# Start of a fused attention and feed-forward kernel: warm-up matmuls, halved first loads, and another order of the weight loads

## The chip, the core and the metric

The kernel runs on one core of a Trainium2 chip. The metric is the device time of one execution in microseconds (us). The core has five engines with their own instruction streams: TensorE (PE; its weight loads are listed as PEld), VectorE (DVE), ScalarE (ACT), GpSimd (POOL) and SyncE (SP). DMAs are issued by POOL or SP and are carried by the core's 16 DMA engines.

## The reference

```python
def _attn_ref(q, k, v):                       # q, k, v: (8, 8, 576, 64)
    scores = np.matmul(q, k.transpose(0, 1, 3, 2)) / np.sqrt(64)
    rel = pos[:, None] - pos[None, :]
    mask_plain = (rel >= 0) & (rel < 32)                          # heads 0 to 3
    mask_dil = (rel >= 0) & (rel < 128) & (rel % 4 == 0)          # heads 4 to 7
    scores = np.where(mask, scores, -1e9)
    attn = softmax(scores)
    return np.matmul(attn, v)

x = attn_out.transpose(0, 2, 1, 3).reshape(4608, 512)
h = x @ w_in                                  # 512 x 2048
g = h * sigmoid(beta * h)
out = g @ w_out                               # 2048 x 512
```

All inputs and the output are float32; the kernel computes its products in bfloat16.

## The kernel before

The work has two halves. Attention is done for one batch of 576 tokens at a time and leaves its result, transposed, in `xT`. The feed-forward part runs over nine tiles of 512 tokens (`NTT`). Its weights stay in SBUF: `w_in_bf` is loaded in four DMAs of 512 columns, `w_out_bf` in four quarters of 512 rows. Every load that casts from float32 to bfloat16 is issued by POOL.

Attention is cut into small steps whose order is written out by hand as lists of names: `FIRST` for batch 0, `SECOND` for batch 1, `THIRD` for batch 2 and `STEPS` for the others. In a name the letter is the kind and the digits are the head pair and the part. Head pairs 0 and 1 are the plain ones, 2 and 3 the dilated ones.

- `K` and `Q` (batches 0 and 1 only) transpose rows of k and q, which lie with tokens on partitions in `tok`, by TensorE into PSUM, and copy them out (`transposes_d`, `transposes_p`, `step_k`, `step_q`).
- `S` computes a block of scores and its exponential on ScalarE. For batches 0 and 1 the mask is added by a matmul with `neg_d` or `neg_p`; later batches multiply by a mask on POOL.
- `V` multiplies with the values and divides by the sums on VectorE. `X` transposes the result and ScalarE copies it into `xT`.
- `v0` and `v1` cast the two parts of the dilated values from `vd_st` into `vd`, `v2` casts the plain values from `vp_st` into `vp` (`cast_v`). `H0` and `H1` start the first two feature blocks of tile 0 from the half of `xT` that is there.

For batches 2 to 7, q and k take another way: POOL issues a DMA that casts them into a scratch tensor in DRAM (`cast_qk`, the tensor `qk`), and SP then issues DMA transposes of it (`load_dil`, `load_plain`), which are spread into place by copies (`d`, `k`, `q` in the lists).

The main loop goes over the nine tiles. A tile has 16 slots `slot_h` (four matmuls on `w_in_bf`, a tanh on ScalarE, then `g` on VectorE) and 16 slots `slot_o` (token block `tb`, part 0 to 3; a part is four matmuls on one quarter of `w_out_bf`). Between the slots of tile t stand the attention steps of batch t + 1. In tile 0 the steps of batch 1 begin after the tenth slot, and the order of the `slot_o` is part by part, so that each quarter of `w_out_bf` is used by three token blocks before the next one is needed:

```python
left = [(slot_o, 0, tb, part) for part in range(4) for tb in range(3)] + left[12:]
```

Every engine works through its instructions in the order in which they are written. POOL's order before the main loop is: the loads of batch 0 (dilated k and q, dilated v, plain k and q, plain v) with the identity and the `neg` masks in between, `w_in_bf`, the cast `v2`, the first two quarters of `w_out_bf`, the loads of batch 1, the two `cast_qk` of batch 2, the last two quarters of `w_out_bf`, then memsets and masks.

Of the kernel before, what the change touches and what calls it, by code (L numbers as in the profile page):

```python
# [20 lines left out]
).split()  # L21

FIRST = (
    "K2 K3 Q2 S20 S21 v0 S22 S23 v1 S30 S31 K0 K1 S32 V20 S33 V21 Q0 V22 V23 S00 V30 "
    "S01 V31 X20 S02 v2 V32 S10 V33 X21 S11 V00 X30 S12 V01 X31 V10 H0 X00 V11 H1 X01 X10 X11"
).split()
SECOND = (
    "K2 K3 Q2 v0 S20 v1 S21 S22 S23 K0 K1 S30 V20 S31 Q0 V21 S32 V22 S33 V23 V30 S00 "
    "V31 X20 v2 S01 V32 S02 V33 S10 X21 S11 V00 X30 S12 V01 X31 V10 X00 V11 X01 X10 X11"
).split()  # L30
THIRD = (
# [6 lines left out]
def kernel(  # L38
# [10 lines left out]
    nc = tc.nc  # L49
# [15 lines left out]
    NFB = DFF // P  # L65
    NTOK = 512
    NTT = B * S // NTOK
    WG = 512
    FROM = {1: 2}
    DV = D + 2  # L70
    NEG = 1e9
# [19 lines left out]
    def bank(dt=FP32):  # L91
        b = psum_at.tile([P, 512], FP32, name="at")
        return b[:] if dt == FP32 else b[:].bitcast(BF16)
# [35 lines left out]
    for n, x in ((n, x) for x in (1, 0) for n in "kq"):  # L129
        R, T = (48, 12) if x else (64, 9)  # L130
        tok[n, x] = xT[0:R, :, c:c + T * D]
        c += T * D
    warm = const([P, 1], FP32, "warm")
    gate_t = const([1, 16], BF16, "gate_t")


# [2 lines left out]
            nc.gpsimd.memset(kz[i][64:128, :, :, 0], 0.0)  # L139
            nc.gpsimd.memset(kz[i][0:64, :, :, 1], 0.0)  # L140

    def zeros(i):
        if i == 0:
            for x in range(4):
                nc.vector.memset(pt[x][:, pt_w[x]:], 0.0)
            for x in range(2, 4):
                nc.vector.memset(pt[x][64:96, 8 * DQ[0]:8 * DQ[0] + 32], 0.0)
        nc.vector.memset(qzd[i][64:128, 0], 0.0)
        nc.vector.memset(qzd[i][0:64, 1], 0.0)
        nc.vector.memset(vd[i][:, :, :, :, D:D + 1], 1.0)  # L150
        nc.vector.memset(k1[i][:, :, 0:WIN], 0.0)
        nc.vector.memset(q1[i][64:128, :, 0], 0.0)
        nc.vector.memset(q1[i][0:64, :, 1], 0.0)
        nc.vector.memset(vp[i][:, :, :, D:D + 1], 1.0)


    def band(flat, w, lo, hi, yes, no):
        nc.gpsimd.memset(flat, yes)
        if len(flat.shape) == 2:
            flat = flat.unsqueeze(1)  # L160
        r = flat.shape[1]
        nc.gpsimd.affine_select(
            out=flat, in_=flat, pattern=[[0, r], [1, w]], base=-lo,
            channel_multiplier=-1, compare_op=ALU.is_ge, fill=no)
        nc.gpsimd.affine_select(
            out=flat, in_=flat, pattern=[[0, r], [-1, w]], base=hi,
            channel_multiplier=1, compare_op=ALU.is_ge, fill=no)
# [4 lines left out]
    def build_neg_d():  # L172
        for hf, lo in enumerate(LO):
            band(neg_d[hf][:], DQ[hf], -lo, WIN - 1 - lo, 0.0, -NEG)


    def build_neg_p():
        band(neg_p[:], QT, -WIN, -1, 0.0, -NEG)
        nc.gpsimd.memset(neg_p[0:WIN, 0], -NEG)
# [28 lines left out]
        nc.vector.tensor_single_scalar(  # L208
            out=beta_half[:], in_=tpb[:, 0:NFB], scalar=0.5, op=ALU.mult)

    def load_w_in(g):
        nc.gpsimd.dma_start(
            out=w_in_bf[:, :, g * WG:(g + 1) * WG],
            in_=moe_w_in[:, g * WG:(g + 1) * WG].rearrange("(c p) d -> p c d", p=P))

    def load_w_out(g):
        nc.gpsimd.dma_start(
            out=w_out_bf[:, g * 4:(g + 1) * 4, :],
            in_=moe_w_out[g * 4 * P:(g + 1) * 4 * P, :].rearrange("(c p) d -> p c d", p=P))
# [12 lines left out]

    def load_tok(b, n, x):
        dst = tok[n, x]
        R, T = (48, 12) if x else (64, 9)
        src = {"q": q, "k": k}[n][b, 4 * x:4 * x + 4].rearrange("h (a T) d -> a h (T d)", T=T)
        nc.gpsimd.dma_start(out=dst, in_=src)


    def load_dil(b, kind):
# [18 lines left out]
    def copy_on(eng):  # L261
        return eng.copy if eng is nc.scalar else eng.tensor_copy
# [21 lines left out]
    def load_vp_1(b, eng, n=0, m=4 * NI, p=0):  # L284
        eng.dma_start(
            out=vp_st[b % 2][:].rearrange("p h i d -> p (h i) d")[p:P, n:n + m],
            in_=bass.AP(tensor=v.tensor, offset=v[b, 0].offset + (QT * n - WIN + p) * D,
                        ap=[[D, P - p], [QT * D, m], [1, D]]))
# [11 lines left out]
    def load_vd(b, eng):  # L300
        rows = v[b, 4:8].rearrange("h (t T) d -> t h (T d)", T=C)
        st = vd_st[:].rearrange("p f h T d -> p f h (T d)")
        for hf in range(2):
            eng.dma_start(out=st[0:DK[hf], hf], in_=rows[DO[hf]:DO[hf] + DK[hf]])


    def cast_v(b, n, eng):
        if n == 2:
            copy_on(eng)(out=vp[b % 2][:, :, :, 0:D], in_=vp_st[b % 2][:])
        else:  # L310
            f, K = (slice(n, n + 1), DK[n]) if n < 2 else (slice(0, 2), 96)
            copy_on(eng)(
                out=vd[b % 2][0:K, f].rearrange("p f h T e -> p (f h T) e")[:, :, 0:D],
                in_=vd_st[0:K, f].rearrange("p f h T d -> p (f h T) d"))
# [3 lines left out]
        kd[b] = kd_pool.tile([P, 2, 4, CT], BF16, name="kdT")  # L318


    def transposes_d(n, rp):
        src = tok[n, 1]
        tv = bank(BF16)[:, 0:4 * CT].rearrange("p (h w a) -> p h w a", h=4, w=3)
        for h4 in range(4):
            for w in range(3):
                c = (4 * w + 2 * rp) * D
                nc.tensor.transpose(tv[:, h4, w], src[:, h4, c:c + 2 * D], ident_b[0:48, 0:48])
        return tv.rearrange("p h w a -> p h a w")


    def transposes_p(n, x):
        src = tok[n, 0]
        tv = bank(BF16)[:, 0:S].rearrange("p (e a) -> p e a", e=9)
        for h2 in range(2):
            for e in range(9):
                nc.tensor.transpose(
                    tv[64 * h2:64 * h2 + 64, e], src[:, 2 * x + h2, e * D:(e + 1) * D],
                    ident_b[0:64, 0:64])
        return tv.rearrange("p e a -> p a e")

    def step_k(b, x):
        eng = nc.scalar if x % 2 else nc.vector
        if x < 2:
            copy_on(eng)(out=k1[b][:, x, WIN:].rearrange("p (a e) -> p a e", e=9),
                         in_=transposes_p("k", x))
        else:
            copy_on(eng)(out=kd[b][:, x - 2].rearrange("p h (a w) -> p h a w", w=3),
                         in_=transposes_d("k", x - 2))


    def step_q(b, x):
        tv = [transposes_p("q", y) if y < 2 else transposes_d("q", y - 2) for y in (x, x + 1)]
        for n, hf in ((0, 0), (1, 1), (0, 1), (1, 0)):
            y, rows = x + n, slice(64 * hf, 64 * hf + 64)
            out = (q1[b][rows, y, hf].rearrange("p (a e) -> p a e", e=9) if x < 2 else
                   qzd[b][rows, hf, y - 2].rearrange("p h (a w) -> p h a w", w=3))
            copy_on(nc.scalar if hf else nc.vector)(out=out, in_=tv[n][rows])  # L357

    def step_s(b, x, j):
# [88 lines left out]
            nc.scalar.copy(out=o, in_=xp[:, 0:m * n].rearrange("p (T t) -> p T t", T=C))  # L448

    STEP = {"K": step_k, "Q": step_q, "S": step_s, "V": step_v, "X": step_x}  # L450
    BRING = {"d": spread_dil, "k": spread_k, "q": spread_q, "v": cast_v}

    def attention_step(b, name):
        if name[0] == "H":
            slot_h(0, int(name[1:]), (2, 3))
        elif name[0] in STEP:
            STEP[name[0]](b, *[int(c) for c in name[1:]])
        else:
            eng = (nc.scalar if name[0] == "v" and (b, name) in ((1, "v2"), (2, "v0"), (2, "v1"), (2, "v2")) else
                   nc.gpsimd if b == 0 and name == "v2" else nc.vector)  # L460
            BRING[name[0]](b, int(name[1:]), eng)


# [97 lines left out]
    def gate(element):  # L561
        G.tensor_copy(out=gate_t[0:1, 0:1], in_=element)

    V.memset(warm[:], 0.0)
    A.activation(out=warm[:], in_=warm[:], func=ACT.Exp)
    V.memset(vp_st[0][0:WIN, 0, 0], 0.0)
    SQ.dma_start(out=beta_row[:], in_=moe_beta.rearrange("(f p) -> f p", p=P))
    for n in "kq":
        load_tok(0, n, 1)
    make_identity(nc, ident_b[:])  # L570
    load_vd(0, G)
    load_tok(0, "k", 0)
    build_neg_d()
    load_tok(0, "q", 0)
    load_vp_1(0, G, 0, 1, WIN)
    load_vp_1(0, G, 1, 4 * NI - 1)
    build_neg_p()
    for g in range(4):
        load_w_in(g)
    make_identity(nc, ident_f[:])  # L580
    zeros(0)
    for name in FIRST:
        if name == "S11":
            build_beta()
        attention_step(0, name)
    for g in range(2):
        load_w_out(g)
    for x in (1, 0):
        for n in "kq":
            load_tok(1, n, x)  # L590
    G.memset(vd_st[64:96, 1], 0.0)
    load_vd(1, G)
    load_vp_1(1, G)
    for kind in "kq":
        cast_qk(2, kind)
    zeros(1)
    V.memset(plain_T["k"][:, 0:WIN // 2], 0.0)
    for kind in "kq":
        load_dil(2, kind)
    for kind in "kq":  # L600
        load_plain(2, kind)
    for g in range(2, 4):
        load_w_out(g)
    zeros_kz()
    build_masks_d()
    build_masks_p()
# [68 lines left out]
```

## Time and profile before

| | |
|---|---|
| median of 11 runs | 341.63 us (340.9 to 344.13) |
| the profiled execution | 341.39 us |
| its span, first to last instruction | 339.7 us |
| PE busy | 311.1 us (92%) |
| DVE, ACT, POOL busy | 193.3, 197.6, 130.4 us |
| moved by DMA | 42.61 MB, mean 125 GB/s |
| matmul of 128x512 on `w_in_bf` (line 475) | 380 ns, 520 of them |
| matmul of 128x512 on `w_out_bf` (line 508) | 379 ns, 512 on `o_ps` |
| first instruction of PE | 6.72 us |
| PE idle for a DMA, total | 8.3 us for k, 0.9 us for q, 3.1 us for `w_out_bf` |

A duration is that of one instruction. Matmuls overlap in the array: four on `w_out_bf` in a row end 1.02 us after the first starts, and 0.86 us lie between the starts of two such groups. Times in the text are counted from the first instruction of the span; the device time is 1.7 us longer than the span.

### The profile page before, as it was taken

How to read it: one execution, taken by the hardware profiler on the slowest of the kernel's cores; microseconds unless marked ns; L12 is line 12 of the kernel's file. 1: busy time of each engine (PE TensorE's matmuls, PEld its weight loads, DVE VectorE, ACT ScalarE, POOL GpSimd, SP SyncE). 2: the span in 40 equal slices, each digit the busy share in tenths (PEclk: the TensorE clock that was granted, in tenths of full speed). 3: DMA queues.
4: the chain of work that ended last, by engine and by line, in shares of the span. 5: the costliest groups of instructions: out<-in, count | busy, mean ns of one | idle time of the engine just before them, and what ended most of it. 6: DMA issues, size and time to landing. Idle time of an engine off the chain costs nothing.

```text
span 339.7 us, 6278 instructions
## 1 busy us (share of the span) xinstructions
PE 311.1 (92%) x2389; PEld 165.7 (49%) x2389; DVE 193.3 (57%) x424; ACT 197.6 (58%) x374; POOL 130.4 (38%) x170
## 2 busy tenths in 40 slices
PE   1889796997899899999999999999999999999994
PEld 1754463544455455555555555555555444444441
DVE  4588663479657774767386637763865344244400
ACT  2577564686747675666666656665666555355411
POOL 8773594133385346534653465354434000000000
PEclk9999999999999999999999999999999999999999
DMA  7999999999899695979688968892001210011121
GB/s 107 209 206 207 181 229 169 211 209 201 147 162 166 125 188 112 172 181 131 133 140 185 125 134 153 172 126 63 20 13 33 62 33 32 32 31 34 41 82 62
DMA packets 64734, 42.61 MB, mean 125 GB/s; under 512 B 48832, under 2 KB 58976, under 8 KB 64320
## 3 DMA queue, kind: packets, MB, share of 16 engines
q1 hardware_dynamic: 57120, 25.58, 40.0%
q0 software_dynamic: 7584, 16.64, 27.9%
q8 instruction: 18, 0.29, 0.4%
q14 instruction: 12, 0.10, 0.1%
HBM read 39.32 MB, written 16.52 MB: 164 GB/s over the span
## 4 chain that ended last, share of the span: by engine, by line
PE 75%; DMA 12%; DVE 5%; ACT 4%; issue 1%; POOL 1%; ACTq 0%; POOLq 0%
PE o_ps L508 31%; PE h_ps L475 29%; DMA xT<-in_q_dram 7%; DMA w_out_bf<-in_moe_w_out_dram 5%; PE h_ps L508 3%; PE at L417 3%; PE at L434 2%; PE at L391 2%; PE at L384 2%; ACT osb L513 2%; DVE g L485 2%; DVE qq L278 1%; ACT tnh L482 1%; DVE xs L424 1%; POOL pt L399 1%
## 5 line engine op out<-in xcount | busy, mean ns | idle before, releaser
L485 DVE SCALAR_TENSOR_TENSOR g<-tnh,h_ps 128x512 bf16<-128x512 bf16 x130 | 88.8, 685 | 90.4 <-ACT tnh L482 89.6
L475 PE MATMUL h_ps<-xT,w_in_bf 128*128 128x512 bf16 x520 | 131.2, 380 | 2.5 <-DVE g L485 2.1
L508 PE MATMUL o_ps<-w_out_bf,g 128*128 128x512 bf16 x512 | 128.9, 379 | 3.8 <-ACT osb L513 3.8
L482 ACT ACTIVATE tnh<-h_ps,beta_half 128x512 bf16<-128x512 f32 x130 | 89.3, 687 | 56.3 <-PE h_ps L475 51.8
L508 PEld LDWEIGHTS <-g 128*128 128x128 bf16 x576 | 52.3, 97 | 57.4 <-issue 8.3
L475 PEld LDWEIGHTS <-w_in_bf 128*128 128x128 bf16 x576 | 51.8, 98 | 51.5 <-issue 3.5
L397 ACT ACTIVATE pt<-at 128x384 bf16<-128x384 f32 (+2 forms) x112 | 48.4, 439 | 20.8 <-PE at L384 8.5
L399 POOL TENSOR_TENSOR pt<-pt,mask_d 96x384 bf16<-96x384 bf16 (+1 forms) x48 | 36.9, 778 | 52.3 <-ACT pt L397 51.7
L424 DVE TENSOR_TENSOR xs<-at,rcp 96x256 bf16<-96x256 f32 (+2 forms) x96 | 44.5, 463 | 12.3 <-PE at L434 8.4
L399 POOL TENSOR_TENSOR pt<-pt,mask_PP 128x384 bf16<-128x384 bf16 x24 | 22.8, 948 | 37.8 <-ACT pt L397 37.7
L513 ACT ACTIVATE osb<-o_ps 128x512 f32<-128x512 f32 x32 | 19.1, 597 | 23.7 <-PE o_ps L508 23.6
L417 PEld LDWEIGHTS <-pt 128*128 128x128 bf16 (+2 forms) x448 | 24.5, 97 | 13.5 <-DVE xs L424 0.2
L420 DVE RECIPROCAL rcp<-at 96x4 f32<-96x4 f32 (+2 forms) x96 | 16.8, 175 | 8.4 <-PE at L417 7.7
L391 PEld LDWEIGHTS <-kdT 128*96 128x96 bf16 (+1 forms) x128 | 15.3, 127 | 11.9 <-issue 2.3
L391 PE MATMUL at<-qzd,kdT 128*96 128x192 bf16 (+1 forms) x128 | 19.0, 236 | 1.6 <-ACT qzd L357 0.8
L434 PE MATMUL at<-ident_b,xs 96*128 96x96 bf16 (+1 forms) x224 | 18.0, 200 | 1.3 <-DVE xs L424 1.2
L434 PEld LDWEIGHTS <-xs 96*128 96x128 bf16 (+1 forms) x224 | 13.2, 96 | 11.4 <-DVE xs L424 1.9
L417 PE MATMUL at<-vd,pt 96*128 96x65 bf16 (+1 forms) x256 | 18.3, 193 | 0.0
L508 PE MATMUL h_ps<-w_out_bf,g 128*128 128x512 bf16 x64 | 15.5, 379 | 3.1 <-DMA w_out_bf<-in_moe_w_out_dram 3.1
L399 POOL TENSOR_TENSOR pt<-pt,mask_FP 128x384 bf16<-128x384 bf16 x12 | 10.9, 910 | 16.0 <-ACT pt L397 16.0
L448 ACT COPY xT<-at 128x384 bf16<-128x384 bf16 (+1 forms) x32 | 12.6, 394 | 3.9 <-PE at L434 3.9
L444 ACT COPY xT<-at 128x288 bf16<-128x288 bf16 x24 | 9.0, 399 | 10.0 <-PE at L434 10.0
(89 smaller groups left out, 225.3 us busy)
## 6 DMA issues: line engine op xcount, KB each, us to landing
vp_st<-in_v_dram SPq DMA_DIRECT2D x12, 384.0 KB, 8.8
qk<-in_k_dram POOLq DMA_DIRECT2D x6, 576.0 KB, 5.7
qk<-in_q_dram POOLq DMA_DIRECT2D x6, 576.0 KB, 8.7
vd_st<-in_v_dram SPq DMA_DIRECT2D x6, 384.0 KB, 5.2
w_in_bf<-in_moe_w_in_dram POOLq DMA_DIRECT2D x4, 512.0 KB, 11.5
w_out_bf<-in_moe_w_out_dram POOLq DMA_DIRECT2D x4, 512.0 KB, 16.3
out_dram<-osb SPq DMA_DIRECT2D x8, 256.0 KB, 2.6
vd_st<-in_v_dram SPq DMA_DIRECT2D x6, 320.0 KB, 6.4
```

Of the source, the lines that this page charges most:

```text
L391: nc.tensor.matmul(sc[0:K, a, 0:2 * n], lhsT=kd[b][:, rp, h4, DO[hf]:DO[hf] + K], rhs=qzd[b % 2][:, :, rp, h4, hf * DQ[0]:hf * DQ[0] + n], ...
L397: nc.scalar.activation(out=w, in_=sc[0:K, :, 0:2 * n], func=ACT.Exp, scale=SCALE)
L399: nc.gpsimd.tensor_tensor(out=w, in0=w, in1=mask[0:K], op=ALU.mult)
L417: nc.tensor.matmul(pv[:, a, h2, :], lhsT=pt[x][0:K, c:c + P], rhs=rhs, start=True, stop=True)
L420: nc.vector.reciprocal(out=rcp[0:n, 0:m], in_=pv[0:n, :, :, D])
L424: nc.vector.tensor_tensor(out=xs_t[b, x, jx][:, a0:a0 + m], in0=pv[0:n, :, :, 0:D], in1=rcp[0:n, 0:m].unsqueeze(3).to_broadcast([n, m, 2, ...
L434: nc.tensor.transpose(xp[:, a * n:(a + 1) * n], xs[:, a].rearrange("p h d -> p (h d)"), ident_b[0:n, 0:n])
L475: nc.tensor.matmul(hps, lhsT=w_in_bf[:, kt, fb * P:(fb + 1) * P], rhs=xT[:, kt, t * NTOK:(t + 1) * NTOK], start=(kt == 2), stop=(kt == 1))
L482: nc.scalar.activation(out=tnh[:], in_=hps, func=ACT.Tanh, scale=beta_half[:, fb:fb + 1])
L485: nc.vector.scalar_tensor_tensor(out=g[:], in0=tnh[:], scalar=1.0, in1=hps, op0=ALU.add, op1=ALU.mult)
L508: nc.tensor.matmul(ops[:], lhsT=g_t[t, fb][:, tb * P:(tb + 1) * P], rhs=w_out_bf[:, fb, :], start=(fb == 0), stop=(fb == NFB - 1))
L513: nc.scalar.mul(out=osb[:], in_=ops[:], mul=0.5)
```

## The change

1. Matmuls on a tile of zeros (`W10`, `W2`, `W3` and `W2` in `FIRST`, 17 in all) are issued on TensorE before and between the first transposes.
2. The dilated k and q of batch 0 are loaded in two DMAs each, by head pair. `K2`, `Q2`, `K3` and `Q3` become steps of one head pair each, for batch 0 and batch 1, and their copies are half as large.
3. All memsets of VectorE that were spread over two places come first, apart from `z0`, `z1` and `z2`. The memsets of the `neg` masks go from POOL to VectorE.
4. `w_in_bf` is loaded in pieces of 256, 256, 512 and 1024 columns, issued after the cast `v1`, which moves from VectorE to POOL for batch 0. The last piece is issued after the first half of the plain values is cast.
5. The plain values of batch 0 are loaded and cast in two parts (`v4`, `v5`) in place of `v2`, both on POOL.
6. The quarters of `w_out_bf` are issued between the loads of batch 1: the first after its dilated q and k, the second after its plain q and k, the third after its dilated values, and the last after the casts and transposes of batch 2.
7. The lists `FIRST` and `SECOND` are in a new order.

The core of the diff:

```diff
 FIRST = (
-    "K2 K3 Q2 S20 S21 v0 S22 S23 v1 S30 S31 K0 K1 S32 V20 S33 V21 Q0 V22 V23 S00 V30 "
-    "S01 V31 X20 S02 v2 V32 S10 V33 X21 S11 V00 X30 S12 V01 X31 V10 H0 X00 V11 H1 X01 X10 X11"
+    "W10 K2 W2 Q2 W3 K3 S20 S21 Q3 W2 S22 S23 z0 v0 S30 S31 S32 S33 V20 V21 K0 v1 V22 V23 V30 K1 X20 "
+    "V31 Q0 V32 V33 X21 S00 X30 S01 X31 S02 v4 S10 V00 S11 V01 S12 H0 v5 X00 V10 H1 X01 V11 X10 X11 z1 z2"
 ).split()
 SECOND = (
-    "K2 K3 Q2 v0 S20 v1 S21 S22 S23 K0 K1 S30 V20 S31 Q0 V21 S32 V22 S33 V23 V30 S00 "
+    "K2 Q2 K3 Q3 v0 S20 v1 S21 S22 S23 K0 K1 S30 V20 S31 Q0 V21 S32 V22 S33 V23 V30 S00 "
     "V31 X20 v2 S01 V32 S02 V33 S10 X21 S11 V00 X30 S12 V01 X31 V10 X00 V11 X01 X10 X11"
 ).split()
...
+    warm_w = const([P, 512], BF16, "warm_w")
+    warm_ps = psum_o.tile([P, HD], FP32, name="o_ps")
...
+    def zeros():
+        nc.vector.memset(warm_w[:], 0.0)
+        nc.vector.memset(warm[:], 0.0)
+        for hf in range(2):
+            nc.vector.memset(neg_d[hf][:], 0.0)
+        nc.vector.memset(neg_p[:], 0.0)
...
+    def zeros_q(b, n, eng):
+        t = qzd[1] if n == 1 else q1[n // 2]
+        eng.memset(t[64:128, 0] if n == 1 else t[64:128, :, 0], 0.0)
+        eng.memset(t[0:64, 1] if n == 1 else t[0:64, :, 1], 0.0)
...
+    def load_tok(b, n, x, h0=0, nh=4):
...
+        nc.gpsimd.dma_start(out=tok[n, x][:, h0:h0 + nh], in_=src)
...
+        if name[0] == "W":
+            for n in range(int(name[1:])):
+                nc.tensor.matmul(warm_ps[:], lhsT=warm_w[:, 0:P], rhs=warm_w[:], start=True, stop=True)
...
+    zeros()
...
     for n in "kq":
-        load_tok(0, n, 1)
+        load_tok(0, n, 1, 0, 2)
     make_identity(nc, ident_b[:])
+    for n in "kq":
+        load_tok(0, n, 1, 2, 2)
     load_vd(0, G)
...
-    load_vp_1(0, G, 1, 4 * NI - 1)
-    build_neg_p()
-    for g in range(4):
-        load_w_in(g)
-    make_identity(nc, ident_f[:])
-    zeros(0)
+    load_vp_1(0, G, 1, 2 * NI - 1)
+    load_vp_1(0, G, 2 * NI, 2 * NI)
     for name in FIRST:
-        if name == "S11":
+        if name == "v1":
+            attention_step(0, "v1")
+            build_neg_p()
+            for c0, c1 in ((0, 256), (256, 512), (512, 1024)):
+                load_w_in(c0, c1)
+            continue
+        if name == "v5":
+            load_w_in(1024, 2048)
+            make_identity(nc, ident_f[:])
+        if name == "X10":
             build_beta()
         attention_step(0, name)
-    for g in range(2):
-        load_w_out(g)
-    for x in (1, 0):
+    for x, g in ((1, 0), (0, 1)):
         for n in "kq":
             load_tok(1, n, x)
+        load_w_out(g)
     G.memset(vd_st[64:96, 1], 0.0)
     load_vd(1, G)
+    load_w_out(2)
     load_vp_1(1, G)
...
-    for g in range(2, 4):
-        load_w_out(g)
+    load_w_out(3)
```

## The prediction

> **What bounds the kernel now.** I read the page's busy shares and its chain first, then the chain in order of time, then a table by stage, then the DMA issues with their times to landing.
>
> ```profile
> PE 311.1 (92%) x2389; PEld 165.7 (49%) x2389; DVE 193.3 (57%) x424; ACT 197.6 (58%) x374; POOL 130.4 (38%) x170
> ...
> PE 75%; DMA 12%; DVE 5%; ACT 4%; issue 1%; POOL 1%; ACTq 0%; POOLq 0%
> ```
>
> TensorE is busy 311.1 of 339.7 us: 28.6 us idle is all that any reordering can win. The table by stage (columns: stretch, length, then busy us of PE, PEld, DVE, ACT, POOL, granted clock, DMA share, GB/s) says where it lies.
>
> ```profile
> 0.00:23.00 23.00, 13.42 (x219) 11.02 (x219) 13.10 (x42) 11.32 (x25) 18.25 (x36) 1.00 1.00 171
> 23.00:37.00 14.00, 11.70 (x90) 5.70 (x86) 11.55 (x26) 9.54 (x18) 5.05 (x7) 1.00 1.27 196
> 37.00:44.00 7.00, 6.88 (x70) 3.75 (x68) 4.54 (x7) 4.97 (x9) 5.07 (x6) 1.00 1.17 193
> 44.00:54.20 10.20, 10.16 (x145) 6.69 (x144) 6.73 (x17) 5.53 (x13) 9.46 (x16) 1.00 1.05 212
> 54.20:66.30 12.10, 8.96 (x93) 5.41 (x93) 4.52 (x15) 6.76 (x15) 1.91 (x6) 1.00 1.18 202
> 66.30:99.00 32.70, 28.89 (x228) 15.25 (x225) 23.01 (x49) 22.90 (x43) 13.64 (x16) 1.00 1.04 186
> ```
>
> Length minus PE, summed to 66.3: 9.6 + 2.3 + 0.1 + 0.0 + 3.1 = 15.2 us idle, with the DMA engines full throughout. After 66.3 only 13.4 us are lost over 273 us, and the change does not edit that part. The first 66 us are a DMA stage. The chain shows which transfer ends it:
>
> ```profile
> 21.62 16.88 DMA xT<-in_q_dram
> 38.50 0.28 issue
> 38.79 18.41 DMA w_out_bf<-in_moe_w_out_dram
> 57.19 0.04 issue
> 57.23 1.02 PE h_ps L508 x4
> ```
>
> The wait at its end, from the list of PE's waits between 54 and 67 us, is the only one there:
>
> ```profile
> PE h_ps L508 <- DMA w_out_bf<-in_moe_w_out_dram: 3.1, 1, 3.1
> ```
>
> The DMA issues of that stretch (KB, then us from issue to landing; the first from the window 36 to 40, the second from 40 to 46):
>
> ```profile
> w_out_bf<-in_moe_w_out_dram POOLq DMA_DIRECT2D x1, 512.0 KB, 18.4
> w_out_bf<-in_moe_w_out_dram POOLq DMA_DIRECT2D x1, 512.0 KB, 20.2
> ```
>
> They are issued at 38.79 and 40.00, so they land at 57.2 and 60.2: twenty us after issue, because POOL's queue serves in order. Issue plus landing time for each DMA of POOL gives the queue's clock: second batch's first plain v 48.8, qk of k 51.2, qk of q 53.9, third quarter of w_out 57.2, last quarter 60.2. Differences are service times: 2.5, 2.7, 3.2, 3.0; of the first w_out quarter 2.5, of a q/k load of 288 KB 1.2 to 2.1.
>
> **The change, part by part.** *Order of the weights.* The third quarter of w_out goes from behind the two qk casts to ahead of plain v. It then lands after w_in (28.7), four q/k loads (7.0 together), two quarters (2.5 + 3.2) and vd (3.4): about 44.8, plus 2.6 for itself, 47.4. The 3.05 us wait at 57.23 goes. What is late next: plain v of batch 1 lands 2.6 later, 51.4 for 48.8. Its cast v2 is on ScalarE, started at 54.26 and will be reached some 2.6 us earlier, at 51.6; behind it on ScalarE queue the exponentials of S01 to S12, which PE's V steps wait for; about even. The qk casts land at 53.9 and 56.6, and SP's transposes (issued 51.24 and 53.97 on those landings) go 2.6 us later. In the before they crawl beside w_out and land at 60.8 to 64.2; later they have only one quarter to crawl beside, so I expect about 60.5 to 64.5. SP then issues the v loads of batch 2 as now (62.17).
>
> *What ends the stage.* Last in the queue is still a quarter of w_out. The bytes ahead are the same, so it cannot land much earlier than 60.2: I take 59.6, since both late quarters ran at 3.2 and 3.0 beside the transposes against 2.5, and only one of them still does (bounds 59.0 and 60.7). PE's first use of it, the first part-3 group, was at 62.04. The three part-3 groups with their S, V and X steps ran from 62.04 to 66.28 and PE was busy 4.14 of these 4.24 us, so they will take 4.2 again. Tile 1 then starts at 59.6 + 4.2 = 63.8 against 66.28: 2.4 us gained. PE must arrive at part 3 before 59.6: without its 3.05 wait it would have come at 59.0 with nothing else gained. So the gain stands even if every other edit wins nothing, and nothing won there counts either, as a new wait of 0.6 to 3 us before part 3 takes it.
>
> *Zero matmuls and half loads.* Seventeen matmuls of 512 columns are added. Before 14 us a 384-column matmul follows the next by 0.32 us (starts 11.39 and 11.71) and after that by half of it (the granted clock reads 1.00 in both, so here durations tell); 512 columns cost 0.43 cold and 0.215 warm (four in 0.86). Ten of them cost 4.3 us, from 1.3 (a memset of 256 words, about 0.25 by the 0.54 for 576) to 5.6. PE was idle to 6.72. The first half of k lands at half of the first load: between 4.8 and 5.8. The other seven (1.5 to 3.0 us) lie in waits for the other halves. Cost of all on the path 0 to 0.8 us, taken as 0; the cover is the DMA queue, and with it gone the 0.8 shows. The half loads add two DMAs, 0.55 us of POOL each by the 24 KB row; bytes are equal. S20 can start about 2 us earlier. The first attention ends perhaps 3 us earlier, tile 0 starts at 23 instead of 25.8, K2 of batch 1 finds its rows at about 31 without its 1.6 us wait (it comes before the quarters of w_out now). Then VectorE's v0 waits for vd at 42.8 with the last g of tile 0 and K0's copy queued behind it, and PE's Q0 for the bank that K0's copy frees. That gives most of it back: Q0 at 46 against 48.46. Part 3 is then reached at about 56.5 and waits 3 us.
>
> *POOL.* v1 moves to POOL (1.46 us for 1536 columns, so 0.97 for 1024) and plain v takes two casts of 0.73 for one of 1.46. neg_p and w_in now stand behind v1, which waits for vd at 11.7; w_in's first issue moves from 11.32 to about 14.1. The first issue took 1.50, so its packets flow at about 16.4, and plain v keeps the queue full to 18.0. Slack 1.6 us, cost 0. The band memsets move to VectorE, which is done before 4.5 as before. w_in in 256, 256, 512 and 1024 columns: same bytes; unit cost of 512 columns was 2.4 to 3.1 us; estimate from -0.5 to +0.7, taken as 0. The last half is needed by feature block 8, about 30 us, and lands at 28.7. The z memsets (six of 0.54 each) move off the gap before the first g; z1 and z2 stay there. Value 0 to 1 us, hidden by the same queue.
>
> [...] The trace: after the 3.05 us wait four matmuls of w_out took 1.02 us, as those without a wait do. [...] The new wait before part 3 is estimated at 0.6 to 3.1 us, so by the row it costs nothing. [...]
>
> *Sum.* The profiled execution took 341.39 us with a span of 339.7; minus 2.4 gives 339.0. The median of the eleven runs is 0.24 above the profiled one: 339.2. Some of the 2.4 may reappear between 66 and 99, where loads of batch 2 and 3 now have less time in front of their users; I allow 0.1 and say 339.3.
>
> **The rivals.** *Half of it is lost again (340.9).* [...] Chance 0.15.
>
> *More than that (337.8).* If the last quarter lands at 59.0 and the casts overlap better, PE saves 3.0, and up to 0.6 comes from the VectorE waits at 80 to 82 us. Chance 0.15.
>
> *Slower (343.0).* POOL's v1 cast starves the queue. w_in stands behind a cast that waits for vd. If vd lands 1.6 us later than 11.7, or the cast and neg_p take 1.6 longer, the queue runs dry at 18.0, and each us more goes straight to the last quarter at 59.6 and to the end. It decides from 1.6 + 2.4 = 4.0 us of delay on; 5.5 us would give 343.0. Against: the trace shows no cast on POOL longer than 1.9 us and POOL had 2.8 us of idle just there. Chance 0.10.
>
> *The change does nothing (341.5).* If the three final transfers merely swap and the last one lands at 62, as transposes now run beside it alone, part 3 is no earlier. Chance 0.05. The forecast keeps 0.55.
>
> **How the numbers follow.** About 0.3% (1.0 us) is what a measurement of this kernel can tell from no change, so faster means below 340.6. Forecast and better case are faster, of the half-lost case a third: 0.55 + 0.15 + 0.05 = 0.75. Same: the rest of it and the case of nothing, 0.15. Slower 0.10. The likeliest alone spans 338.2 (landing 59.0, and 0.4 more) to 340.3 (landing 60.7). The range for 8 in 10 goes from 337.9 to 341.4.
>
> **What would show it.** Right: no wait of PE on w_out at the first part-2 group; instead one on the last quarter before part 3, at 59 to 60.5, of 0.6 to 3 us; tile 1's first matmul at 63 to 65; the table of stages alike from there. K2 of batch 1 without a DMA wait; v0 of batch 1 waiting on VectorE. Wrong: a gap in the DMA row between 16 and 20 us; 384-column matmuls at 0.5 after 60 us; a wait of d0, v0 or the kz copies on their loads at 68 to 80.

## The result and the profile after

The changed kernel takes 340.01 us (median of 13 runs, 338.33 to 342.63), the kernel before 342.33 (50 runs, 340.85 to 344.59). The ratio is 0.993 with a 95% interval of 0.9908 to 0.9953: between 1.6 and 3.1 us faster. Twelve more runs (`changed_again`, below) gave 0.9914 (0.9881 to 0.9948). The profiled execution took 339.96 us with a span of 338.2; it is 1.43 us shorter than the profiled one of before (341.39), and the steps below are measured against that number.

The page of the changed kernel: busy shares, the granted clock in 40 slices, the chain.

```profile
PE 318.4 (94%) x2406; PEld 168.5 (50%) x2406; DVE 194.5 (58%) x433; ACT 198.1 (59%) x380; POOL 131.3 (39%) x172
...
PEclk9959999999999999999999999999999999999998
...
PE 82%; DVE 7%; ACT 5%; DMA 2%; POOL 2%; issue 1%; POOLq 0%; ACTq 0%
```

DMA's share of the chain fell from 12% to 2%. TensorE is busy 7.3 us longer, of which the 17 matmuls on zeros are 6.4 (their group's total). The third digit of PEclk is a 5, half clock, where the page of before has a 9. The table by stage, in the columns and nearly the cuts of before:

```profile
0.00:23.00 23.00, 18.58 (x224) 12.09 (x225) 12.99 (x49) 10.86 (x26) 18.19 (x37) 0.84 1.01 163
23.00:37.00 14.00, 13.29 (x88) 6.92 (x86) 10.86 (x22) 9.78 (x17) 6.20 (x9) 0.90 1.22 196
37.00:44.00 7.00, 6.89 (x73) 3.71 (x73) 5.52 (x11) 4.85 (x12) 5.75 (x6) 1.00 1.18 220
44.00:54.20 10.20, 9.55 (x138) 6.50 (x137) 7.13 (x15) 5.77 (x13) 9.26 (x18) 1.00 1.08 234
54.20:66.30 12.10, 11.58 (x114) 6.85 (x113) 5.21 (x17) 8.49 (x19) 1.20 (x3) 1.00 1.16 201
66.30:99.00 32.70, 28.37 (x227) 15.02 (x226) 23.57 (x50) 22.91 (x43) 14.72 (x16) 1.00 0.99 180
```

In the fifth row, which held the 3.05 us wait, TensorE is now busy 11.58 of 12.10 us. The first two rows have the clock at 0.84 and 0.90: there part of the busy time is longer instructions: a 384-column matmul takes 0.50 to 0.52 us at a clock of 0.50 (19.62 to 24.17) and 0.33 at 1.00 (8.38). TensorE's four longest waits of the first 70 us (what it waited for: us in total, times, longest):

```profile
PE at L352 <- DMA xT<-in_k_dram: 1.4, 1, 1.4
PE o_ps L475 <- DVE neg_d L147: 1.3, 1, 1.3
PE at L436 <- DVE vd L323: 1.1, 1, 1.1
PE h_ps L530 <- DVE g L507: 0.6, 1, 0.6
```

The second is the start of the first matmul on zeros. None of them is on `w_out_bf`: the 3.05 us wait for the third quarter is gone, and no wait for the last one has come. The row of the last quarter among the DMA issues (window 38.7 to 39.5; issued at 39.20) puts its landing at 58.0:

```profile
w_out_bf<-in_moe_w_out_dram POOLq DMA_DIRECT2D x1, 512.0 KB, 18.8
```

The third quarter was issued at 32.72 and landed 14.6 us later, at 47.3. TensorE came to part 2 at 55.18 and to part 3 at 59.98, each time after the quarter was there.

The runs below are compared by the marks of this table, all in us, read from the profiled executions. Tile 0 and tile 1: start of their first full group on `w_in_bf`; part 0 (its first and second group), part 2, part 3: start on that quarter of `w_out_bf`; last quarter: its landing; rest: span minus tile 1; half clock: stretches with the granted clock at 0.5, without the one with which each record ends. Cold start: the record of the clock begins there, and a 384-column matmul takes 0.50 to 0.55 us before it and 0.32 to 0.34 after it; the mean granted clock of an execution leaves this part out. Cold starts that end before 7.2 us are not listed.

```
                     tile 0  part 0  second  part 2  part 3  last qu. tile 1  rest    half clock
before                25.79   43.75   45.84   57.23   62.04   60.19    66.28  273.4   (cold start to 14.84)
changed               27.96   44.23   46.83   55.18   59.98   58.02    64.97  273.3   15.57-25.82
old_order             26.80   45.06   48.44   58.16   62.97   61.24    67.95  273.3   16.45-23.28
no_zero_mm            27.98   44.24   48.12   58.02   62.83   59.46    67.82  273.3   49.13-52.55 (cold to 25.24)
order_only            27.71   44.03   46.39   54.56   59.37   56.67    63.61  273.4   (cold to 23.14)
vd_first              28.10   44.38   46.80   55.15   59.96   59.43    64.95  273.3   15.42-25.66
w_in_512              28.32   44.59   47.42   55.77   60.58   58.70    65.56  273.3   15.67-25.91
busy_vd_first         25.35   41.62   44.95   53.31   58.12   57.97    63.10  273.2   none
order_busy            24.46   40.78   44.98   54.81   59.62   56.33    63.87  273.5   45.37-48.78
before_busy           24.67   46.29   48.38   57.27   62.08   60.32    66.32  274.6   37.91-44.74, 82.28-85.70
order_busy_vd         24.39   40.71   43.51   51.68   56.98   56.94    61.22  273.4   none
order_busy_vd_late    24.66   42.69   44.61   52.74   57.55   57.07    61.79  273.4   none
changed_again         27.08   43.35   46.25   54.60   59.41   56.59    64.40  273.3   14.79-25.03
```

The column "rest" carries the reading of everything else: after tile 1 starts, 273.2 to 273.5 us follow in each kernel (274.6 in the one that drops to half clock there). All the other differences are made before.

### The profile page after: what moved, and what is told of

Its sections match the earlier page's. It is cut to its first block, busy times and chain, and to the rows that moved or that the text cites. A ratio compares the mean times of both kernels' runs of the same rounds, so it can differ in the third digit from the quotient of the medians.

```text
span 338.2 us, 6328 instructions
## 1 busy us (share of the span) xinstructions
PE 318.4 (94%) x2406; PEld 168.5 (50%) x2406; DVE 194.5 (58%) x433; ACT 198.1 (59%) x380; POOL 131.3 (39%) x172
## 4 chain that ended last, share of the span: by engine, by line
PE 82%; DVE 7%; ACT 5%; DMA 2%; POOL 2%; issue 1%; POOLq 0%; ACTq 0%
PE o_ps L530 32%; PE h_ps L497 30%; PE h_ps L530 4%; PE at L436 3%; DVE g L507 3%; PE at L453 3%; PE at L497 3%; DMA xT<-in_k_dram 2%; PE at L403 2%; ACT osb L535 2%; PE at L410 2%; ACT tnh L504 2%; PE at L391 1%; PE at L352 1%; DVE xs L443 1%
## 5 line engine op out<-in xcount | busy, mean ns | idle before, releaser
L497 PEld LDWEIGHTS <-w_in_bf 128*128 128x128 bf16 x576 | 51.9, 98 | 51.4 <-issue 3.1
L416 ACT ACTIVATE pt<-at 128x384 bf16<-128x384 f32 (+2 forms) x112 | 47.7, 439 | 18.5 <-PE at L403 8.0
L418 POOL TENSOR_TENSOR pt<-pt,mask_d 96x384 bf16<-96x384 bf16 (+1 forms) x48 | 36.9, 777 | 51.4 <-ACT pt L416 50.8
L410 PEld LDWEIGHTS <-kdT 128*96 128x96 bf16 (+1 forms) x128 | 14.3, 120 | 10.6 <-issue 1.2
L410 PE MATMUL at<-qzd,kdT 128*96 128x192 bf16 (+1 forms) x128 | 17.9, 227 | 0.8 <-DVE qzd L276 0.8
L403 PEld LDWEIGHTS <-kz 128*128 128x128 bf16 x144 | 9.9, 97 | 9.0 <-issue 2.0
```

The costliest lines, as they stand in the source:

```text
L410: nc.tensor.matmul(sc[0:K, a, 0:2 * n], lhsT=kd[b][:, rp, h4, DO[hf]:DO[hf] + K], rhs=qzd[b % 2][:, :, rp, h4, hf * DQ[0]:hf * DQ[0] + n], ...
L416: nc.scalar.activation(out=w, in_=sc[0:K, :, 0:2 * n], func=ACT.Exp, scale=SCALE)
L418: nc.gpsimd.tensor_tensor(out=w, in0=w, in1=mask[0:K], op=ALU.mult)
L497: nc.tensor.matmul(hps, lhsT=w_in_bf[:, kt, fb * P:(fb + 1) * P], rhs=xT[:, kt, t * NTOK:(t + 1) * NTOK], start=(kt == 2), stop=(kt == 1))
```

## The experiments

Every kernel here computes the full result; matmuls on zeros only add work. Ratios are to the kernel before on the same chip, with 95% intervals.

**Which part carries the gain?** Four kernels: the order of the weights alone, the change without that order, the change without its zero matmuls, and the change with more of them.

`order_only`, the kernel before with one edit:

```diff
-    for g in range(2):
-        load_w_out(g)
-    for x in (1, 0):
+    for x, g in ((1, 0), (0, 1)):
         for n in "kq":
             load_tok(1, n, x)
+        load_w_out(g)
...
     load_vd(1, G)
+    load_w_out(2)
...
-    for g in range(2, 4):
-        load_w_out(g)
+    load_w_out(3)
```

> The kernel before with one edit: the quarters of w_out go between the loads of batch 1, the last one after the casts of batch 2; nothing else changes. Theory A (the order of the weights carries the gain): PE no longer waits for w_out at the first part-2 group; the last quarter lands at 58 to 60, tile 1 starts at 62.5 to 64.5 instead of 66.3, and the time falls by 2 to 3.5 us, as much as with the whole change or more, with the clock at full from 15 us on. Theory B (the zero matmuls and half loads carry it): less than 1 us.

Measured: 338.76 us (338.48 to 339.67), ratio 0.9915 (0.9882 to 0.9948). This edit alone gives as much as the whole change does: the intervals overlap. Its part 3 starts at 59.37, 2.7 us after the last quarter landed.

`old_order`, the changed kernel with this edit undone.

> The changed kernel with the old order of the weights: quarters one and two of w_out before the loads of batch 1, three and four after the casts of batch 2. Theory A: PE waits for the third quarter at 57 again, tile 1 starts at 66 to 67, and the time is that of the kernel before or up to 1 us above, 342 to 343. Theory B: the gain of 2.3 us stays, 340.

Measured: 343.80 us (342.08 to 347.71), ratio 1.0041 (1.0017 to 1.0064): slower than before. The wait on the third quarter is back with 1.2 us at 58.16. In this order all other edits together cost time, and the new order of the weights pays for them.

`no_zero_mm`, the changed kernel with W10, W2, W3 and W2 taken out of `FIRST`.

> The changed kernel without its 17 matmuls on zeros. Theory A: they win nothing at the end, so 339.5 to 340.5 us, within 1 us of the changed kernel; if the half-clock stretch of 10 us seen there between 15.6 and 25.8 us comes from an early start of the clock that is lost in the next waits, it is gone or shorter here, the granted clock is 0.99 or more, and the time is up to 1.5 us lower. Theory B: 1 to 2 us slower than the changed kernel, as the first attention runs at half clock for longer.

Measured: 340.25 us (339.54 to 344.07), ratio 0.9964 (0.9943 to 0.9985). The interval overlaps that of the change (0.9908 to 0.9953), so a gain from the zeros inside the change, some 0.3% by the middle values, is not settled. In the traces tile 0 starts at the same time with and without them (27.96 and 27.98). Its profiled execution (342.83 us, one of its longer ones) waits 1.9 us for a `g` before the second group of part 0, up to 48.12, and at 49.13 the clock drops. In the row of that stretch the clock, third number from the end, is 0.83:

```profile
44.00:54.00 10.00, 8.07 (x106) 5.38 (x105) 6.10 (x8) 4.05 (x9) 9.39 (x14) 0.83 1.12 241
```

`keep_busy`, the changed kernel with 17 more zero matmuls where TensorE waits in the first attention:

```diff
-    "W10 K2 W2 Q2 W3 K3 S20 S21 Q3 W2 S22 S23 z0 v0 S30 S31 S32 S33 V20 V21 K0 v1 V22 V23 V30 K1 X20 "
-    "V31 Q0 V32 V33 X21 S00 X30 S01 X31 S02 v4 S10 V00 S11 V01 S12 H0 v5 X00 V10 H1 X01 V11 X10 X11 z1 z2"
+    "W10 K2 W2 Q2 W3 K3 S20 S21 Q3 W2 S22 S23 z0 v0 S30 S31 S32 S33 W5 V20 V21 W6 K0 v1 V22 V23 V30 K1 X20 "
+    "V31 W3 Q0 V32 V33 X21 W3 S00 X30 S01 X31 S02 v4 S10 V00 S11 V01 S12 H0 v5 X00 V10 H1 X01 V11 X10 X11 z1 z2"
```

> The changed kernel with 17 more matmuls on zeros, put into PE's waits between 11 and 20 us: five before V20, six before K0, three before Q0, three before S00. Theory A2 (the half-clock stretch makes PE late, so that it and no longer the DMA queue sets the start of tile 1): no half-clock stretch after 6 us, tile 0 starts at 25 to 26 instead of 28, PE waits again for the last quarter of w_out at about 58, tile 1 starts at 62.3 to 63, and the time is 1.5 to 2.7 us below the changed kernel, 337.3 to 338.5. Rival: the stretch is hidden by the DMA queue; the time is within 0.5 us of the changed kernel.

Measured: 337.6, 337.78 and 338.23 us, ratio of these 0.9883 (0.9841 to 0.9925), and 344.24 us in the profiled execution. As that one is no picture of the other three, the table leaves it out and no time is taken from its trace. What it shows is seen again in the kernels below: a first attention without half clock, and then a wait for a `g`, with the cast of the dilated values `vd` ahead of that `g` on VectorE.

**What stands behind that wait, and what delays the queue?** The load of `vd` goes ahead of the second quarter of `w_out`:

```diff
     for x, g in ((1, 0), (0, 1)):
         for n in "kq":
             load_tok(1, n, x)
-        load_w_out(g)
+        if g == 0:
+            load_w_out(g)
     G.memset(vd_st[64:96, 1], 0.0)
     load_vd(1, G)
+    load_w_out(1)
     load_w_out(2)
```

`vd_first` is the changed kernel with this edit, `busy_vd_first` is `keep_busy` with it.

> The changed kernel with one transfer moved: the dilated values of batch 1 are loaded before the second quarter of w_out, not after it. Theory A3 (VectorE stands at v0 until these values land, the last g of tile 0 stands behind it, and PE waits for the buffer that this g frees): the values land at about 42 instead of 44 to 45, PE's wait on g (0.6 us in the profile of the changed kernel, 1.4 to 3.0 in its variants) is gone, and the time is 0.5 to 1.5 us below the changed kernel, 338.5 to 339.5. Rival: the clock's half-speed stretch at 16 to 26 us makes PE come later than the values anyway; within 0.3 us of the changed kernel.

> The kernel with 34 matmuls on zeros and the dilated values of batch 1 ahead of the second quarter of w_out. Theory A2 with A3: tile 0 starts at 25.5 to 26, no wait on g, no half-clock stretch before the end, PE waits for the last quarter of w_out at 58 to 59.5, tile 1 starts at 62.3 to 63.5; 337 to 338 us. Rival: v0 still stalls VectorE by 2 us or more and the clock falls after it; 338 to 339 with a wide spread.

Measured: `vd_first` 339.76 us, ratio 0.9905 (0.9877 to 0.9934), no different from the change; there the wait for the `g` was 0.6 us and is 0.5. `busy_vd_first` 338.11 us, ratio 0.986 (0.9833 to 0.9887). No stretch of half clock is left, but the wait, which was expected to go, is 1.4 us, although the values land at 40.59 and VectorE starts the cast only at 42.71. So in these two kernels a late load is not what stands behind the wait. Its row of the first attention and its wait:

```profile
14.00:26.00 12.00, 11.04 (x180) 7.57 (x179) 8.81 (x26) 7.40 (x17) 10.72 (x18) 1.00 1.19 206
```

```profile
PE h_ps L530 <- DVE g L507: 1.4, 1, 1.4
```

`order_busy` is `order_only` with zero matmuls: `warm_w`, a memset of it first on VectorE, the `W` branch, and

```diff
-    "K2 K3 Q2 S20 S21 v0 S22 S23 v1 S30 S31 K0 K1 S32 V20 S33 V21 Q0 V22 V23 S00 V30 "
+    "W12 K2 K3 W4 Q2 W3 S20 S21 v0 S22 S23 v1 S30 S31 K0 K1 S32 V20 S33 V21 Q0 W3 V22 V23 W3 S00 V30 "
```

> The kernel before with the new order of the weights and 25 matmuls on zeros in PE's waits of the first 18 us; the first loads, the casts, w_in and the memsets stay as before. Theory A2: with the clock held, tile 0 starts at 25 to 26 instead of 27.7, the last quarter of w_out lands at 56.7 as with the order alone, and tile 1 starts at 61.5 to 62.5; 336.5 to 337.7 us, 1 to 2 below the order alone. Rival (the zeros win nothing because VectorE's wait for the dilated values gives it back): 338.5 to 339, as the order alone.

Measured: 338.19 us (337.32 to 339.05), ratio 0.9854 (0.9828 to 0.9881). Tile 0 starts at 24.46, 3.25 us earlier than in `order_only`, but tile 1 is no earlier (63.87 against 63.61). A wait of 1.8 us for a `g` stands in between, and one stretch of 3.41 us at half clock after it. That profiled execution took 339.03 us at a clock of 0.992; three of those at 0.995 to 0.997 took 337.3 to 337.6, the fourth 339.05. Against `order_only` the zeros gain some 0.6% by the ratios, whose intervals all but meet; what this execution won at tile 0 it lost in the wait and the stretch behind it.

`w_in_512`, the changed kernel with `w_in` in four equal pieces as before, asks whether the small pieces delay the queue.

> The changed kernel with w_in in four pieces of 512 columns at the same places of the queue. If the pieces of 256 and 1024 columns cost DMA time, all of w_in lands 0.3 to 0.6 us earlier than 30.4 and the time is 0 to 0.5 us lower; if the delay of the queue comes from the half loads and from the start of the stage, w_in still ends at 30 or later and the time is that of the changed kernel, 340.

Measured: 339.51 us, ratio 0.9888 (0.9855 to 0.9921). `w_in` then ended at 31.21 against 30.42 in the changed kernel. The pieces are not the cause.

**Zeros without the order, and all that helped together.** `before_busy` is the kernel before with the zero matmuls of `order_busy` and the weights in their old order.

> The kernel before with 25 matmuls on zeros in PE's waits of the first 18 us and nothing else: the order of the weights stays. Theory A (the first 66 us end with the DMA queue, so an earlier first attention alone wins nothing): tile 0 starts at 24.5 to 25 instead of 25.8, PE waits for the third quarter of w_out at 57 as before, and tile 1 starts at 66 to 67; 0 to 0.5 us from the kernel before. Theory B (the zeros have a gain of their own): 1 us or more faster.

Measured: 341.78 us (340.01 to 342.63), ratio 0.9976 (0.9953 to 0.9998). Tile 0 starts 1.1 us earlier than before, and tile 1 at 66.32 against 66.28. The first lines of its waits from 20 to 70 us:

```profile
PE at L329 <- DMA xT<-in_k_dram: 2.4, 1, 2.4
PE h_ps L513 <- DMA w_out_bf<-in_moe_w_out_dram: 0.5, 1, 0.5
```

The gain at tile 0 ran into the wait for the second batch's k (up to 36.32), the clock fell after it (37.91 to 44.74), and the third quarter still ended the stage at 57.27. While the queue sets the end, a faster TensorE gains next to nothing: here 0.2% with an interval that ends at 0.02%. (Two of its twelve executions kept full clock; they took 340.01 and 341.04 us.)

`order_busy_vd` is `order_busy` with the edit of `vd_first`. `order_busy_vd_late` moves the casts too:

```diff
 SECOND = (
-    "K2 K3 Q2 v0 S20 v1 S21 S22 S23 K0 K1 S30 V20 S31 Q0 V21 S32 V22 S33 V23 V30 S00 "
+    "K2 K3 Q2 S20 S21 S22 S23 K0 v0 K1 S30 V20 v1 S31 Q0 V21 S32 V22 S33 V23 V30 S00 "
```

> The kernel before with the new order of the weights, 25 matmuls on zeros, and the dilated values of batch 1 ahead of the second quarter of w_out. Theory A3: these values land at 39.5 to 41 instead of 42 to 43.5, PE's wait of 1.8 us behind g shrinks to below 1 and the half-clock stretch of 3.4 us after it is gone; tile 1 starts at 61 to 62.5 and the time is 0.5 to 1.5 us below the same kernel without the move, 336.8 to 337.7.

> As the kernel with the dilated values ahead of the second quarter of w_out, and v0 and v1 of batch 1 later in the list, v0 behind K0 and v1 behind V20, so that no g stands behind them on VectorE. Theory A3: no wait of PE on g; PE waits instead at V20 or for the last quarter of w_out at 56.5, tile 1 starts at 60.8 to 62; 336.3 to 337.3 us. Rival: V20 comes later by what g comes earlier, and nothing is won against the kernel without this edit.

Measured: `order_busy_vd` 336.66 us (336.11 to 337.71), ratio 0.9838 (0.9804 to 0.9873); `order_busy_vd_late` 336.93 us, ratio 0.9842 (0.9809 to 0.9874). Moving the casts gives nothing more; TensorE then waits 1.0 us for a copy of q. These two are the fastest versions found, ahead of both kernels. Against `order_busy` the interval of the first still overlaps; in the traces its tile 1 starts 2.65 us earlier (61.22 for 63.87). Three views of the first: the first attention and the stretch of the parts, the wait, and part 3.

```profile
14.00:26.00 12.00, 10.84 (x161) 7.65 (x159) 9.85 (x33) 8.17 (x20) 7.55 (x12) 1.00 1.18 207
...
44.00:54.00 10.00, 9.98 (x121) 6.30 (x120) 5.59 (x17) 5.92 (x12) 8.25 (x17) 1.00 1.06 229
```

```profile
PE h_ps L513 <- DMA w_out_bf<-in_moe_w_out_dram: 0.3, 1, 0.3
```

```profile
56.98 1.02 PE L513 MATMUL h_ps<-w_out_bf,g 128*128 128x512 bf16 x4 [0.33 <-DMA w_out_bf<-in_moe_w_out_dram]
```

The clock holds, and TensorE waits for the last quarter before part 3. That is the end of the stage which the prediction named; neither trace of the changed kernel reached it.

`changed_again` is the changed kernel, run beside these.

> The changed kernel as it is, beside the other three on one chip. Theory A2: a half-clock stretch between about 15 and 26 us again in the profile, a granted clock of 0.975 to 0.990 in its executions, 338.3 to 341 us, and the time falls as the clock rises. Rival: the stretch was a chance of one execution, and the profile shows full clock from 6 us on.

Measured: 339.65 us (338.03 to 341.48), ratio 0.9914 (0.9881 to 0.9948). It has the same 10.24 us at half clock, so that stretch is no accident of one execution.

## Why the prediction was right, and where it was wrong

**The order of the weights: right, and it is the gain.** The third quarter was put at 47.4 and landed at 47.3, and the 3.05 us wait went. Plain v landed at 49.9 for 51.4, the qk casts at 52.5 and 55.2 for 53.9 and 56.6, the transposes from 59.2 to 63.4 for 60.5 to 64.5. The loss of any of these later on did not come: the rest took 273.3 us, as before. K2 of batch 1 found its rows without a wait, as forecast. `order_only` and `old_order` show that this edit alone makes the sign.

**What ends the stage: wrong, in a way that nearly cancels.** The prediction had the last quarter land at 59.6 and TensorE wait for it from 56.5. It landed at 58.0, below the lower bound of 59.0, and TensorE came at 59.98 and did not wait. So the start of part 3 was 0.4 us off although both terms were off, by 1.6 and by 3.5.

Behind the first stands the step "the bytes ahead are the same, so it cannot land much earlier". The bytes were the same, but the queue served them faster. From the landing of all of `w_in` to that of the last quarter it took 31.5 us before (28.67 to 60.19) and 27.6 in the changed kernel (30.42 to 58.02): the four q and k loads of batch 1 took 5.6 us for 7.0, its plain v 2.6 for 3.9, the third quarter 2.4 for 3.2. In the tables by stage the DMA engines moved 220 and 234 GB/s in the third and fourth rows, where they moved 193 and 212 before. With the old order of the weights the same stretch is 31.8 us in `before_busy` and 31.9 in `old_order`; in all kernels of the table with the new order it is 27.0 to 28.4. So the faster queue comes with the order; why is not shown. It also makes the 47.3 of the third quarter luck in part: `w_in` was 1.75 us late, and the q and k loads behind it made up most of that.

Then three part-3 groups took 4.99 us where 4.2 were carried over from before. The end of that stretch, in the changed kernel:

```profile
63.03 1.02 PE L530 MATMUL o_ps<-w_out_bf,g 128*128 128x512 bf16 x4
63.89 0.42 PE L453 MATMUL at<-ident_b,xs 96*128 96x96 bf16 x6
64.83 0.30 PE L453 MATMUL at<-ident_b,xs 96*128 96x96 bf16 x3 [0.52 <-DVE xs L443]
64.97 1.04 PE L497 MATMUL h_ps<-xT,w_in_bf 128*128 128x512 bf16 x4
```

and in the kernel before:

```profile
64.89 1.03 PE L508 MATMUL o_ps<-w_out_bf,g 128*128 128x512 bf16 x4
65.75 0.70 PE L434 MATMUL at<-ident_b,xs 96*128 96x96 bf16 x6
66.28 0.81 PE L475 MATMUL h_ps<-xT,w_in_bf 128*128 128x512 bf16 x3
```

Three more transposes stand between the last group and tile 1, behind a wait of 0.52 us for their input. In tile 0 the slots take steps by count (`first(n)`), and the new `SECOND` has one name more, Q3: each later step slides back by one count, and X01 joins X10 and X11 behind the last slot. In the table all kernels with the new `SECOND` need 4.98 or 4.99 us here, all with the old order of K3 and Q2 4.24 or 4.25. That is 0.75 us of cost the prediction did not see; no run put the old list into the changed kernel. Sum: part 3 was 0.38 late and the groups took 0.79 more than 4.2, which is the 1.17 by which tile 1 is late (64.97 for 63.8).

**"The gain stands even if every other edit wins nothing": the step that failed.** It left out that another edit can lose. From the second group of part 0 to part 3 TensorE needs 13.15 us in both kernels (45.84 to 62.04 less the wait of 3.05; 46.83 to 59.98). So part 3 came 0.99 us later than the 59.0 of "nothing else gained", because the second group of part 0 came 0.99 us later. The next two points are what the traces show behind that.

**Zero matmuls and half loads at cost 0: wrong.** Tile 0 was to start at 23; it started at 27.96, and at 25.79 before. TensorE's timeline, with the granted clock in two-us windows around it:

```profile
8.38 0.33 PE L391 MATMUL at<-neg_d,ident_b 96*96 96x384 bf16 x1
...
12.36 0.42 PE L436 MATMUL at<-vd,pt 96*128 96x65 bf16 x8 [1.14 <-DVE vd L323]
14.16 0.65 PE L352 MATMUL at<-ident_b,xT 64*64 64x64 bf16 x18 [1.39 <-DMA xT<-in_k_dram]
...
20.56 0.52 PE L391 MATMUL at<-neg_p,ident_b 128*128 128x384 bf16 x1
```

```profile
12.00:14.00 2.00, 0.42 (x8) 0.29 (x8) 1.41 (x5) 0.00 (x0) 0.92 (x1) 1.00 1.36 190
14.00:16.00 2.00, 1.84 (x50) 1.69 (x51) 1.11 (x3) 0.00 (x0) 1.79 (x6) 0.89 1.08 216
16.00:18.00 2.00, 1.82 (x41) 1.68 (x42) 1.82 (x8) 1.02 (x2) 1.42 (x2) 0.50 1.09 200
```

With the zeros the record of the clock begins at 5.33, at full speed (a 384-column matmul takes 0.33 at 8.38); without them (`no_zero_mm`) it begins at 25.24. Then TensorE waited 1.14 us for the cast of `vd` and 1.39 for plain k, was busy 0.42 us between 12 and 14, and from 15.57 to 25.82 had half the clock (0.52 for 384 columns), a stretch in which it was busy 9.58 of 10.20 us (15.60 to 25.80). So the clock was full over these waits and half over the work behind them. `busy_vd_first` fills those two waits with more zeros and has full clock throughout: tile 0 at 25.35, so 2.6 us of the 27.96 go with the stretch. Even that is 2.35 later than 23; what holds the rest was not taken apart. `order_busy`, with the old loads and zeros, has 24.46, so nothing speaks for a gain from the half loads.

The 25.79 of before was itself a good case. `order_only` issues the same work in the same order up to 25 us, but its clock rose at 23.14 where that of before rose at 14.84, and its tile 0 starts at 27.71.

A falling clock was looked for at the wrong place. The prediction looked after 60 us (384-column matmuls at 0.5), behind a new wait before part 3; that wait did not come, and the clock fell 44 us before part 3, after the two waits of 1.14 and 1.39 us. The half-lost case's 340.9 and the range hold a loss of 1.7 us to a falling clock, an estimate of the author's that no run shows. What the runs showed in its place is the 10.24 us at half clock of the changed kernel, with 2.6 us at the start of tile 0.

**The casts: half seen.** The prediction had `v0` wait on VectorE for the dilated values, with a `g` and the copy of K0 behind it, priced this on Q0 (46 us; it came at 50.1) and took it as hidden by the queue. In the changed kernel `v0` did not wait: its values had landed at 43.84, and VectorE came to the cast at 45.33, straight from another `g`. But the cast stands ahead of a `g`, and so on the chain:

```profile
44.71 0.61 DVE g L507
45.33 0.86 DVE vd L323
46.18 0.60 DVE g L507
46.83 1.02 PE h_ps L530 x4
```

TensorE waits 0.6 us at the second group of part 0. In other kernels this wait is 1.4 to 1.9 us. One reason is the load: in `order_busy` VectorE sits idle for 1.28 us until it lands. The other thing that the traces show there is POOL, which sets `kz` to zero at this time. The cast in the kernel before, then cast and memset in `order_busy`:

```profile
43.52 0.68 DVE L312 CAST vd<-vd_st 96x1024 bf16<-96x1024 f32 x1
```

```profile
41.91 1.83 DVE L314 CAST vd<-vd_st 96x1024 bf16<-96x1024 f32 x1 [1.28 <-DMA vd_st<-in_v_dram]
41.83 1.37 POOL L141 MEMSET kz<- 64x1536 bf16 x1
```

The same cast takes 0.68 us in one and 1.83 in the other, where it ends 0.54 us after the memset (43.74 and 43.20). It ends 0.55 after one in `no_zero_mm` too (47.48 and 46.93, a cast of 1.97 us) and in `busy_vd_first` (44.31 and 43.76, 1.60 us), and both of these have hardly a wait for the load; in the changed kernel the cast of 0.86 us ends 0.54 after one (46.18 and 45.64). Against the 0.68 of before, the casts in `no_zero_mm` and `busy_vd_first` are 1.29 and 0.92 us longer, the larger part of the 1.9 and 1.4 us that TensorE waits there for the `g`. In the kernel before the cast came first, and the memset behind it took 1.92 us for 1.37. `order_busy_vd` loads the values earlier and starts the cast at 40.47; it still lasts 1.79 us, but the wait for the `g` is 0.4. No run moved the memsets, so that they hold up the cast is the author's reading of these times.

**The rivals.** The one of no effect is excluded by the interval. The slower one, a queue that starves behind `v1`, did not happen as an event, though `w_in` was issued at 15.14 for the 14.1 forecast and ended 1.75 us later than before (30.42 for 28.67): in the row 16 to 18 above the DMA share is 1.09, so the queue had not run dry, and the third quarter of `w_out` came as forecast. The half-lost one did not come: part 3 had no wait before it, and where the clock did fall, at 15.57, it was 44 us earlier.

**The size.** 2.4 us were predicted; the medians differ by 2.3, the two profiled executions by 1.43, of which 1.31 are the earlier start of tile 1. The thirteen executions of the changed kernel lie between 338.33 us at a mean granted clock of 0.990 and 342.63 at 0.975; the profiled one has 0.982. The longer ones have the lower clock, so the half clock goes with this spread, and part of the agreement to 0.7 us is luck. The sign isn't.

## What to carry to other kernels

Move the transfer whose landing ends the stage first; speeding up the engine that waits for it is worth little until then (`before_busy`, 0.2%), and more afterwards (`order_busy_vd`, 0.8% over `order_only` by the ratios). Matmuls on zeros brought tile 0 forward most where full clock lasted up to it (25.35 in `busy_vd_first` and 24.46 in `order_busy`; 26.80 to 28.32 in the kernels with zeros whose clock fell ahead of it, 27.98 without zeros): look for every wait between the last zero and the first dense stretch. A cast placed early in a list holds up the work behind it on its engine: check when its load lands, and what POOL does beside it (0.68 us alone, up to 1.97 beside a memset). And check what one more name does to a list that is dealt out by count.

## What the runs showed of the hardware that was not expected

The stretches at half clock last 3.41, 6.83 or 10.24 us in the table, one, two and three times 3.41; the full clock ahead of the one in the changed kernel lasts 10.24 us too (5.33 to 15.57). Half clock began 1.0 us after the end of a wait of 1.8 us (`order_busy`), 1.0 after one of 1.9 (`no_zero_mm`), 1.6 after one of 2.4 (`before_busy`, the first of its two), and in the changed kernel after two waits of 1.14 and 1.39 us. The 3.05 us wait of before was followed by none, nor the 1.4 us one of `busy_vd_first`. The length of a wait alone does not tell it. TensorE's busy time does not either: the first row below is the 3.41 us ahead of the drop in `order_busy`; the second holds part of the 3.05 us wait of before, which spreads over this stretch and the next one of that length:

```profile
41.96:45.37 3.41, 1.58 (x39) 1.24 (x39) 3.41 (x4) 0.70 (x3) 3.36 (x3) 1.00 1.16 256
```

```profile
52.39:55.80 3.41, 1.79 (x18) 1.10 (x17) 1.19 (x5) 2.40 (x4) 2.29 (x6) 1.00 1.19 197
```

TensorE was busy 1.58 us ahead of that drop, 1.48 ahead of the one of `no_zero_mm`, 1.59 ahead of the first of `before_busy` and 1.83 ahead of the one of the changed kernel. It was busy 1.79 and 1.98 in the two stretches of before, and there the clock held. What makes the clock fall is not shown. Nor is it shown why the same first 25 us came to full clock at 14.84 in before and at 23.14 in `order_only`.

`w_in` ends at 30.42 in the changed kernel and at 28.94 in `order_only`, and the delay is there with the dilated v already (13.0 for the 11.67 of before). It comes neither from the pieces (`w_in_512`) nor from the zeros, as `no_zero_mm` has the dilated v at 12.96 and the end of `w_in` at 31.40. In `changed_again` the dilated v was on time (11.67) and `w_in` ended at 29.59. What holds the queue there stays open.
